# Attention and a max-out feed-forward layer in one kernel: the down product of the last two tiles by Strassen's algorithm, with the output turned

## The chip, the cores and the metric

The kernel runs on one core of one Trainium2 chip. The metric is the device time in microseconds (us) of the whole program, the median of several executions. A profile comes from one execution of its own, with every instruction's engine, start and duration; its span runs from the first to the last instruction.

The engines: TensorE (PE, with its weight loads as PEld) multiplies into PSUM banks; VectorE (DVE), ScalarE (ACT) and GpSimd (POOL) do element-wise work; SyncE (SP) issues the DMA transfers here.

## What is computed

```python
scores = scale * np.matmul(q, k.transpose(0, 1, 3, 2))      # batch 8, heads 8, seq 576, head_dim 64
...
scores = np.where(masks[None, :, :, :], scores, -1000000000.0)   # windows of 32, plain or dilated by 4
...
attn_out = np.matmul(attn, v)                                # softmax in between
x = np.ascontiguousarray(attn_out.transpose(0, 2, 1, 3)).reshape(B * S, H * D)   # 4608 x 512
h = np.maximum(np.maximum(x @ w1, x @ w2), x @ w3)           # 512 -> 768: the up products
return (h @ w_out).astype(np.float32)                        # 768 -> 512: the down product
```

All inputs and the output are float32.

## The kernel before

**Three passes.** A float32 operand is kept as a high part (fp32r, rounded by a cast) and a low part (the operand less its high part). A product takes three passes: high x high, high x low, low x high. So each operand of a product costs a cast (mostly on ScalarE, the helper `copy`, L425) and a subtraction (VectorE or GpSimd, the helper `tt`, L453). Every product below has its factor 3 from this.

**Tiles.** The 4608 tokens go through the feed-forward layer in three tiles of 512 tokens (`plain`) and four of 768 (`fast`), which begin at tokens 1536, 2304, 3072 and 3840. Attention, for 32 units of one batch and a pair of heads, runs ahead of the tiles in between; its output waits in `raw`, a ring of 1152 tokens. It is over before the down product of tile 2304 ends. The scores are the matmuls of L881, the masks L919, the transposes L985, the values matmuls L1041.

**Up product of a fast tile.** Its three weight matrices are multiplied by Strassen's algorithm (Winograd's form), in nine items (feature pair f, matrix g), each of seven products P1 to P7. The halves are: the 512 inputs in two, the tokens in two of 384, the features in pairs of 128. The seven operands on the x side (R11, T1, T2, R21, R22, T3, T4: four quarters and differences) are cast and subtracted once for a tile into `xop`, a part of the tile `wup`. The sums on the weight side were made once, lie in DRAM as `kept_a` and `kept_b`, and are loaded for each item into three buffers `sa` and four buffers `sb` (parts of `wup` and `xs`) that are given out in turn. A product is 6 matmuls (L1415) with a 128x128 block of the weights stationary and 384 tokens moving. The results are combined and taken into the maximum in `hf` (768 features in six blocks of 128 partitions, 768 tokens as columns), by copies on ScalarE and additions and maxima on VectorE.

**Down product of a fast tile.** For six blocks of 128 tokens, `down_part` casts and subtracts 128 columns of all six feature blocks of `hf` into one of two buffers `h` (768 columns wide; the subtraction is mostly on GpSimd). Then 18 matmuls (L1163: six feature blocks, three passes) run with the block of h stationary and the 512 columns of `wdn` (w_out, split when it is loaded) moving, into one bank. ScalarE copies the bank to `o` (L425), and SyncE stores it (L1195). The first block, tokens 384 to 511, is opened ahead of the tile's last up product: four of its feature blocks stand before that product, so that TensorE has work while the last features are finished. The very last bank is copied in two halves, by ScalarE and VectorE.

**What sets the order.** Every step is given to a planner (`Plan`) with a cost for each engine that may do it, its dependences and its buffers. The planner runs through the program with these costs and writes out one order for each engine: feed-forward matmuls follow each other as written, results of the feed-forward layer come first on the other engines (a due time of -1000), and everything else has a due time counted back from the matmul that needs it. Buffers of some kinds are given in turn. The engines then run these orders strictly, each instruction waiting for semaphores.

## Time and profile before

| | |
|---|---|
| median of 3 executions | 657.51 us (656.93 to 657.53) |
| the profiled execution | 657.69 us, of which the span is 655.9 us |
| TensorE busy, share of the span | 644.7 us, 98% |
| VectorE, ScalarE, GpSimd busy | 64%, 46%, 38% |
| DMA | 137.48 MB, 210 GB/s on average |
| mean granted TensorE clock | 0.996 of full speed |

Busy time of TensorE counts a matmul from its first column to its modelled end, so that neighbours overlap; the distance between the starts of matmuls that follow each other tells what one costs. The chain that ended last is followed back from the last instruction: at each step to what released it, or to the instruction before it on its engine. An execution's own time is compared with its own span; the times of two kernels are compared by their medians.

### The profile page before, as it was taken

Reading aid. Unit: us, or ns where it says so; the run is one execution under the profiler, and the core shown is the slowest. Engines: PE = TensorE matmul, PEld = TensorE weight load, DVE = VectorE, ACT = ScalarE, POOL = GpSimd, SP = SyncE. Lnnn points to the kernel's source line nnn. Section 1 sums busy time; section 2 is a strip of 40 time slices with the busy share of each in tenths; the row PEclk is TensorE's granted clock in tenths of the full one; section 3 lists DMA queues with packets and bytes.
Section 4 is the critical chain, followed back from the end, with each engine's and each line's share of the span. In section 5 each row is a group of like instructions: output and inputs, shape, how many; then the busy total and the mean of one; then the engine's idle time right before and its main releaser. Section 6 shows DMA issues by size and latency. Waiting matters only on the chain.

```text
span 655.9 us, 15914 instructions
## 1 busy us (share of the span) xinstructions
PE 644.7 (98%) x6243; PEld 565.8 (86%) x6243; DVE 417.6 (64%) x1224; ACT 300.4 (46%) x909; POOL 248.4 (38%) x284
## 2 busy tenths in 40 slices
PE   8999999999999999999999999999999999999997
PEld 4577778888778878899998899998899998999986
DVE  5688975888969998698877378837033365143320
ACT  4366457545466834535635565235422244322222
POOL 5455585888879943302304222004200014000032
PEclk9899999999999999999999999999999999999999
DMA  9899925546366535987874367674167763377001
GB/s 346 305 363 347 371 80 177 180 146 209 98 217 226 191 129 193 336 304 281 306 243 176 110 225 274 235 253 164 65 226 257 254 229 110 106 279 263 11 33 64
DMA packets 39723, 137.48 MB, mean 210 GB/s; under 512 B 4064, under 2 KB 10720, under 8 KB 35040
## 3 DMA queue, kind: packets, MB, share of 16 engines
q1 hardware_dynamic: 39648, 136.46, 59.1%
q8 instruction: 49, 0.80, 0.5%
q14 instruction: 26, 0.21, 0.1%
HBM read 110.49 MB, written 25.95 MB: 208 GB/s over the span
## 4 chain that ended last, share of the span: by engine, by line
PE 79%; DVE 8%; POOL 5%; DMA 3%; issue 2%; ACT 1%; SPq 0%; POOLq 0%; DVEq 0%; ACTq 0%
PE ffn L1415 40%; PE ffn L1163 20%; PE ffn L1242 10%; PE pair L1041 2%; PE pair L881 2%; POOL s L453 2%; DMA st<-in_w_up_dram 2%; DVE PT L985 2%; DVE W L453 1%; PE pair L627 1%; DMA kept_b<-c 1%; POOL c L453 1%; DVE xs L453 1%; DVE hf L453 1%; DMA fk<-in_qk_p_dram 1%
## 5 line engine op out<-in xcount | busy, mean ns | idle before, releaser
L1415 PE MATMUL ffn<-wup 128*128 128x384 f32 x1026 | 188.1, 335 | 0.0
L1415 PEld LDWEIGHTS ffn<-wup 128*128 128x128 f32 x1026 | 178.5, 188 | 0.8
L453 POOL TENSOR_TENSOR h<-hf,h 128x768 fp32r<-128x768 f32 (+2 forms) x36 | 67.9, 1887 | 267.7 <-ACT h L425 102.5
L1242 PE MATMUL ffn<-xs,wup 128*128 128x512 f32 x648 | 152.1, 393 | 1.4 <-DVE hf L453 1.4
L1163 PE MATMUL ffn<-wdn,h 128*128 128x512 f32 x648 | 152.8, 392 | 0.1
L1242 PEld LDWEIGHTS ffn<-xs,wup 128*128 128x128 f32 x648 | 120.3, 188 | 28.4 <-DVE hf L453 1.8
L1163 PEld LDWEIGHTS ffn<-wdn,h 128*128 128x128 f32 x648 | 120.5, 188 | 25.4 <-DVE h L453 0.6
L985 DVE STREAM_TRANSPOSE PT<-W 32x256 f32<-32x256 f32 (+2 forms) x288 | 109.5, 380 | 16.1 <-PE pair L1041 6.5
L453 DVE TENSOR_TENSOR hf<-ffn,hf 128x384 f32<-128x384 f32 (+1 forms) x108 | 64.8, 600 | 74.1 <-PE ffn L1415 68.4
L1415 PE MATMUL ffn<-wup,xs 128*128 128x384 f32 x486 | 93.8, 335 | 0.0
L931 ACT ACTIVATE W<-W,mx 128x96 f32<-128x96 f32 (+2 forms) x240 | 86.5, 364 | 15.7 <-DVE mx L919 14.3
L1415 PEld LDWEIGHTS ffn<-wup,xs 128*128 128x128 f32 x486 | 85.0, 188 | 0.4
L425 ACT COPY ffn<-ffn 128x384 f32<-128x384 f32 x34 | 15.7, 463 | 90.4 <-PE ffn L1415 90.3
L425 ACT CAST h<-hf 128x768 fp32r<-128x768 f32 (+4 forms) x43 | 30.8, 732 | 54.6 <-PE ffn L1163 34.5
L931 ACT ACTIVATION_READ_ACCUMULATOR W<-W,mx 128x1 f32 (+1 forms) x240 | 45.5, 190 | 0.0
L919 DVE CUSTOM_DVE_ANT_0 W<-pair,steps 128x96 f32<-128x96 f32 (+1 forms) x188 | 36.0, 252 | 13.3 <-PE pair L881 12.0
L453 POOL TENSOR_TENSOR W<-W,sm 128x768 f32<-128x768 f32 (+2 forms) x39 | 37.0, 954 | 19.3 <-DVE sm L960 18.8
L453 DVE TENSOR_TENSOR wup<-raw,wup 128x768 fp32r<-128x768 f32 x28 | 32.8, 1182 | 13.3 <-ACT wup L425 13.2
L955 POOL TENSOR_TENSOR sm<-sm,small_c 128x8 f32<-128x8 f32 (+2 forms) x48 | 12.1, 260 | 65.6 <-ACT W L931 65.0
L453 DVE TENSOR_TENSOR hf<-ffn,u 128x384 f32<-128x384 f32 x12 | 6.7, 558 | 45.9 <-PE ffn L1415 45.8
L425 ACT COPY u<-ffn 128x384 f32<-128x384 f32 x36 | 17.2, 478 | 37.0 <-PE ffn L1415 36.8
L453 POOL TENSOR_TENSOR s<-s,c 128x512 fp32r<-128x512 f32 (+1 forms) x27 | 32.4, 1207 | 3.9 <-ACT c L425 2.7
(113 smaller groups left out, 634.4 us busy)
## 6 DMA issues: line engine op xcount, KB each, us to landing
wup<-kept_a SPq DMA_DIRECT2D x36, 1024.0 KB, 6.0
xs<-kept_b SPq DMA_DIRECT2D x27, 768.0 KB, 4.2
st<-in_w_up_dram SPq DMA_DIRECT2D x18, 512.0 KB, 7.2
out_dram<-o SPq DMA_DIRECT2D x34, 256.0 KB, 2.0
k<-in_qk_d_dram SPq DMA_DIRECT2D x12, 648.0 KB, 4.8
k<-in_qk_p_dram SPq DMA_DIRECT2D x12, 592.0 KB, 5.8
wup<-kept_b SPq DMA_DIRECT2D x9, 768.0 KB, 4.2
kept_a<-wup SPq DMA_DIRECT2D x9, 512.0 KB, 8.3
```

The lines of the kernel that those rows point to most:

```text
L425: nc.scalar.copy(dst, src)
L453: (nc.vector if eng == "dve" else nc.gpsimd).tensor_tensor(dst, a, b, op=op)
L627: nc.tensor.matmul(half(j)[32 * r : 32 * r + nq, 64 * n : 64 * n + 64], qb.t[d, q0 : q0 + nq], kb.t[d, ko + k0 : ko + k0 + 64], start=Fals ...
L881: nc.tensor.matmul(banks[j].t[o : o + nq, 96 * m : 96 * m + nk], kb.t[d, q0 : q0 + nq], kb.t[d, k0 : k0 + nk], start=True, stop=True,)
L919: nc.vector.tensor_tensor_reduce(W.t[rows, a], banks[j].t[rows, 96 * m : 96 * m + nk], mask_of(m)[rows], -0.125, 3e38, ALU.add, ALU.min, m ...
L931: nc.scalar.activation(W.t[rows, a], W.t[rows, a], AF.Exp, bias=mx.t[rows, n : n + 1], scale=-1.0, accum_out=sm.t[rows, n : n + 1],)
L955: nc.gpsimd.tensor_tensor(d, d, eps_c[rows].broadcast_to([d.shape[0], n]), op=ALU.add)
L985: plan.add({"dve": dve(32 * n) + 0.02}, lambda _: nc.vector.transpose(dst(), src()), [*deps, blank], [W, PT])
L1041: nc.tensor.matmul(pv[z].t[64 * j : 64 * j + 64, q : q + c1 - c0], v.t[d, j, y], PT.t[d, 576 * j + 96 * x + c0 : 576 * j + 96 * x + c1], s ...
L1163: nc.tensor.matmul(bank.t, hb.t[:, hz, f], wdn[f].t[:, wz], start=(f == 0 and m == 0), stop=(f == NF - 1 and m == 2), skip_group_check=True,)
L1242: nc.tensor.matmul(bank.t, wup[:, j, wz, 128 * c : 128 * c + 128], xs[:, xz, c, first : first + n], start=(m == 0 and c == EARLY[0]), stop ...
L1415: nc.tensor.matmul(bank.t[:, :n], wb.t[:, w : w + 128], xop[o][:, xz, c], start=start and not m and not c, stop=m == 2 and c == 1, skip_gr ...
```

## The change

For the tiles at 3072 and 3840 (`TURNED`) the down product is done by the same algorithm, with seven products:

- The 768 features are halved by taking the even blocks (0, 2, 4) against the odd ones (1, 3, 5): three pairs q. The 512 outputs are halved in 256 (two blocks e of 128), the tokens in two of 384 (k).
- The weights are stationary and the tokens move: a step is one product for one pair q, 2 blocks e x 3 passes = 6 matmuls of 384 columns. The output has its 512 columns on partitions, so it is turned, goes to an output of its own (`out_t`, 512 x 1536), and is turned back on the host.
- The operands on the h side are cast and subtracted one pair at a time (128 x 384) into `hop`: four buffers, two in each of the two buffers `h`, given in turn. The cast is on ScalarE or GpSimd, the subtraction on VectorE alone. Of the differences, T1 is made in place in `hf`; T2, T3 and T4 are made in buffers that attention no longer needs (`W`, `PT`).
- The sums on the side of the down weights are made once: pairs 0 and 1 after the up products of tile 1536, pair 2 after those of tile 2304 (`down_sums`), stored in DRAM (`kept_d`), and loaded four times for a tile (P5, P6, P3, P7) into the buffers `sb`. P1, P2 and P4 use quarters of `wdn` as they are.
- Two steps of P1 stand before the tile's last up product, as four feature blocks did.
- For tile 3840 the differences of the x side are made apart (`apart`): two of the four go to places of the ring whose tokens are done with, and the first three wait for no operand to be split; its x subtractions may no longer go to GpSimd.
- In the last tile P4 is done for one output block after the other, and the last bank is copied in two halves of 192 columns.

```diff
+TURNED = (3072, 3840)
...
+    KEPT["h"] = [const.tile([128, 2, NF, 128], F32R, name=f"h_{i}") for i in range(2)]
+    KEPT["hop"] = [
+        t.rearrange("p z f n -> p (z f n)")[:, 768 * i : 768 * i + 768].rearrange("p (z n) -> p z n", z=2)
+        for t in KEPT["h"]
+        for i in range(2)
+    ]
...
+    def down_sums(q, after):
...
+        f1, f2 = both(0, c1), both(1, c2)
+        t1 = made(s12, a, c1, z, c2, z, ALU.add, [f1, f2])
+        t3 = made(s34, a, c1, a, c1, z, ALU.subtract, [f1])
+        t2 = made(s12, z, s12, a, c1, a, ALU.subtract, [t1])
+        t4 = made(s34, z, c2, a, s12, z, ALU.subtract, [t2])
...
+        def changed(o, q, x, y, deps):
+            dst = at(0, q, 1) if o == "T1" else SLOTS[3 * q + int(o[1]) - 2]
+            st = plan.add({"dve": dve(n)}, lambda e: tt(e, dst, x, y, ALU.subtract), deps, both=True)
...
+        def split(o, q, src, deps):
+            hop = buf("hop", f"{o}_{t0}_{q}")
+            h = plan.add(
+                {"act": act(n, False), "pool": pool1(n)}, lambda e: copy(e, hop.t[:, 0], src), deps, [hop]
+            )
+            l = plan.add(
+                {"dve": dve(n)},
+                lambda e: tt(e, hop.t[:, 1], src, hop.t[:, 0].bitcast(F32), ALU.subtract),
+                [h],
+                [hop],
+                both=True,
+            )
...
+            def fn(_):
+                for e in es:
+                    for m, (wz, hz) in enumerate(((0, 0), (0, 1), (1, 0))):
+                        nc.tensor.matmul(
+                            bank[e].t[:, :n],
+                            weights(wz, e),
+                            hop.t[:, hz],
...
+            prev = step(prev, "P1", nq - 1, top, True, [])
+            s1 = [copied(f"ds1{t0}_{e}", "o", top[e], prev) for e in E]
...
+            for q in Q:
+                prev = step(prev, "P5", q, mid, True, [])
+            s5 = [copied(f"ds5{t0}_{e}", "tmp", mid[e], prev) for e in E]
+            for q in Q:
+                prev = step(prev, "P6", q, top, False, [x[1] for x in s1])
+            u2 = [copied(f"du2{t0}_{e}", "tmp", top[e], prev) for e in E]
+            for q in Q:
+                prev = step(prev, "P3", q, mid, False, [x[1] for x in s5])
+            for e in E:
+                added(0, 1, e, mid[e], u2[e][0], [prev, u2[e][1]])
+            for q in Q:
+                prev = step(prev, "P7", q, top, False, [x[1] for x in u2])
+            read = [added(1, 1, e, top[e], s5[e][0], [prev, s5[e][1]]) for e in E]
...
+            for q in Q:
+                prev = step(prev, "P2", q, side, True, [])
+            for e in E:
+                added(0, 0, e, side[e], s1[e][0], [prev, s1[e][1]])
...
+            for es in ((0,), (1,)) if last else ((0, 1),):
+                for q in Q:
+                    prev = step(prev, "P4", q, top, False, read, es)
...
             l = plan.add(
-                {"dve": dve(2 * n), "pool": pool(2 * n)},
+                {"dve": dve(2 * n)} if t0 - 2 * n in TURNED else {"dve": dve(2 * n), "pool": pool(2 * n)},
                 lambda e: tt(e, xop[o][:, 1], src, xop[o][:, 0].bitcast(F32), ALU.subtract),
...
+            d1 = sub(block(0, 1), block(0, 1), block(0, 0), [*of(0, 0), *of(0, 1)])
+            d2 = sub(place(0), block(1, 1), block(0, 1), [d1, *of(1, 1), *before])
+            d3 = sub(place(1), place(0), block(0, 0), [d2])
...
+            qs = {2: range(2), 1: range(2, NF // 2)}.get((TURNED[0] - t0) // n, ())
+            plan.kind = "s"
+            kept_down = [*kept_down, *(x for q in qs for x in down_sums(q, ups_end[t0]))]
```

How the order on the engines changes, at three places. Up to the down product of tile 1536 it is the same on all of them. Lines of the helpers move by some numbers (`tt` L453 to L466, the up matmuls L1415 to L1723); the matmuls of `down_part` stay L1163 before and are L1307 after for the turned tiles. `ffn_91` to `ffn_94` before, `ffn_93` to `ffn_96` after, are the same four banks; `h_89` and `h_90` are the two buffers `h`, `W_83` to `W_86` and `PT_87` attention's.

TensorE at the start of the down product of tile 3072, before (x3 is one feature block, x6 one product):

```order
L1415 MATMUL ffn_93<-wup,xs 128x384 x6
L1163 MATMUL ffn_94<-wdn_1227,h_384_6265 128x512 x3
L1163 MATMUL ffn_94<-wdn_1255,h_384_6265 128x512 x3
L1163 MATMUL ffn_94<-wdn_1272,h_384_6265 128x512 x3
L1163 MATMUL ffn_94<-wdn_1296,h_384_6265 128x512 x3
L1415 MATMUL ffn_93<-wup,xs 128x384 x6
L1163 MATMUL ffn_94<-wdn_1304,h_384_6265 128x512 x3
L1163 MATMUL ffn_94<-wdn_1388,h_384_6265 128x512 x3
```

and after, the two opening steps, the last up product, the third step of P1 and the first of P5:

```order
L1723 MATMUL ffn_95<-wup,xs 128x384 x6
L1307 MATMUL ffn_96<-h_89,wdn_1230 128x384 x3
L1307 MATMUL ffn_93<-h_89,wdn_1230 128x384 x3
L1307 MATMUL ffn_96<-h_89,wdn_1274 128x384 x3
L1307 MATMUL ffn_93<-h_89,wdn_1274 128x384 x3
L1723 MATMUL ffn_95<-wup,xs 128x384 x6
L1307 MATMUL ffn_96<-h_90,wdn_1306 128x384 x3
L1307 MATMUL ffn_93<-h_90,wdn_1306 128x384 x3
L1307 MATMUL ffn_94<-h_90,xs 128x384 x3
L1307 MATMUL ffn_95<-h_90,xs 128x384 x3
```

108 matmuls of 512 columns become 126 of 384, in two banks at a time instead of one.

VectorE at the same place, before: the last maxima of the up product, with the x side of tile 3840 (`wup<-raw`: x subtractions, `raw<-raw`: differences):

```order
L453 TENSOR_TENSOR hf<-s_3072_8_6383,hf 128x384
L453 TENSOR_TENSOR wup<-raw,wup 128x768
L453 TENSOR_TENSOR h_384_6265<-hf,h_384_6265 128x256
L453 TENSOR_TENSOR raw<-raw 128x2x384
L453 TENSOR_TENSOR hf<-ffn_93,hf 128x384
L453 TENSOR_TENSOR raw<-raw 128x2x384
L453 TENSOR_TENSOR wup<-raw,wup 128x768
```

and after, from the last up product's maximum on (`hf<-ffn_95,hf`): the four differences of the last pair (T1 in `hf`, T2 and T3 in `W_86`, T4 in `PT_87`), then T1's subtraction, T2's three, and two x subtractions:

```order
L466 TENSOR_TENSOR hf<-ffn_95,hf 128x384
L466 TENSOR_TENSOR hf<-hf 128x384
L466 TENSOR_TENSOR W_86<-hf 128x384
L466 TENSOR_TENSOR W_86<-W_86,hf 128x384
L466 TENSOR_TENSOR PT_87<-hf,W_86 128x384
L466 TENSOR_TENSOR h_89<-hf,h_89 128x384
L466 TENSOR_TENSOR h_90<-W_83,h_90 128x384
L466 TENSOR_TENSOR h_90<-W_84,h_90 128x384
L466 TENSOR_TENSOR h_89<-W_86,h_89 128x384
L466 TENSOR_TENSOR wup<-raw,wup 128x768 x2
```

From here to the end of the down product there stand, in this order: 3 subtractions of R22, an x subtraction, 3 of T3, 2 results, 2 of R21, an x subtraction, 2 results, the third of R21, 3 of T4, 2 results, the x side's last difference and its subtraction. In tile 3840 the queue is the same without the x side, and there T1's subtraction of the last pair stands right behind the last up product's maximum.

VectorE after the down product of tile 1536, after the change: the sums of pair 0, and the first of pair 1 ahead of the first mask instruction of the next attention units (L932). Before, that instruction followed directly on the first row:

```order
L466 TENSOR_TENSOR wup<-raw,wup 128x768
L466 TENSOR_TENSOR dc_0_4817<-wdn_1230 128x512
L466 TENSOR_TENSOR dc_0_4839<-wdn_1258 128x512
L466 TENSOR_TENSOR ds_0_4889<-dc_0_4817,dc_0_4839 128x256
L466 TENSOR_TENSOR ds_0_4889<-ds_0_4889,dc_0_4817 128x256
L466 TENSOR_TENSOR ds_0_4892<-dc_0_4817 128x256
L466 TENSOR_TENSOR ds_0_4892<-dc_0_4839,ds_0_4889 128x256
L466 TENSOR_TENSOR ds_0_4892<-ds_0_4892,dc_0_4839 128x512
L466 TENSOR_TENSOR ds_0_4889<-ds_0_4889,dc_0_4817 128x512
L466 TENSOR_TENSOR dc_1_4961<-wdn_1274 128x512
L932 ISA W_83,mx_4921<-pair_91,steps 128x96
```

The other seven of pair 1 stand among the mask instructions, and TensorE reaches the next scores one up product later and the next values two up products later.

## Rows read from the trace of the kernel before

**Rows 1.** The page's first section: engine, busy us (share), instructions.

```profile
PE 644.7 (98%) x6243; PEld 565.8 (86%) x6243; DVE 417.6 (64%) x1224; ACT 300.4 (46%) x909; POOL 248.4 (38%) x284
```

**Rows 2.** Chain that ended last, in order of time: start us, us, what.

```profile
471.77 64.48 PE ffn L1415 x372
...
540.03 21.77 PE ffn L1163 x96
561.80 64.48 PE ffn L1415 x372
626.28 2.73 PE ffn L1163 x12
629.01 1.04 PE ffn L1415 x6
630.06 21.77 PE ffn L1163 x96
651.90 0.38 ACT o L425
652.30 0.42 DVE o L429
```

**Rows 3.** Busy time in four stretches (columns in the first row).

```profile
core 0: us, PE busy (x) PEld busy (x) DVE busy (x) ACT busy (x) POOL busy (x), PEclk, DMA share, GB/s
376.00:444.00 68.00, 68.00 (x547) 67.22 (x546) 45.28 (x144) 31.68 (x108) 10.39 (x17) 1.00 0.71 245
444.00:472.00 28.00, 28.00 (x215) 23.44 (x214) 13.89 (x15) 12.90 (x25) 10.54 (x5) 1.00 0.31 110
536.09:561.64 25.55, 25.55 (x116) 21.33 (x115) 13.83 (x15) 10.17 (x15) 10.44 (x5) 1.00 0.33 118
626.12:652.00 25.88, 25.70 (x115) 21.14 (x114) 2.40 (x5) 7.12 (x12) 9.26 (x5) 1.00 0.14 52
```

**Rows 4.** VectorE by form, 472 to 652: count, busy us, mean ns, idle before.

```profile
L453 DVE TENSOR_TENSOR hf<-ffn,hf 128x384 f32<-128x384 f32 x36 | 20.1, 558 | 54.7 <-PE ffn L1415 54.2
L453 DVE TENSOR_TENSOR wup<-raw,wup 128x768 fp32r<-128x768 f32 x7 | 8.5, 1227 | 4.2 <-ACT wup L425 4.2
...
L453 DVE TENSOR_TENSOR h<-hf,h 128x256 fp32r<-128x256 f32 x2 | 0.8, 422 | 0.5 <-ACT h L425 0.5
```

**Rows 5.** Timeline, VectorE and GpSimd in the two down products: start us, us, instruction.

```profile
538.86 2.47 POOL L453 TENSOR_TENSOR h<-hf,h 128x768 fp32r<-128x768 f32 x1 [20.95 <-DVE h L453]
...
540.07 0.56 DVE L453 TENSOR_TENSOR hf<-ffn,hf 128x384 f32<-128x384 f32 x1 [0.46 <-PE ffn L1415]
540.54 1.60 DVE L453 TENSOR_TENSOR raw<-raw 128x768 f32<-128x768 f32 x1
...
545.00 0.94 DVE L453 TENSOR_TENSOR raw<-raw 128x768 f32<-128x768 f32 x1
...
625.95 0.56 DVE L453 TENSOR_TENSOR hf<-ffn,hf 128x384 f32<-128x384 f32 x1
626.42 0.55 DVE L453 TENSOR_TENSOR s<-ffn,s 128x384 f32<-128x384 f32 x1
627.01 0.56 DVE L453 TENSOR_TENSOR hf<-s,hf 128x384 f32<-128x384 f32 x1
```

**Rows 6.** ScalarE by form, 626.12 to the end: count, busy us, mean ns, idle.

```profile
L425 ACT CAST h<-hf 128x768 fp32r<-128x768 f32 x5 | 4.2, 835 | 11.0 <-PE ffn L1163 8.3 <-issue 2.8
L425 ACT COPY o<-ffn 128x512 f32<-128x512 f32 x5 | 2.9, 582 | 2.7 <-issue 2.7
...
L425 ACT CAST h<-hf 128x256 fp32r<-128x256 f32 x1 | 0.4, 408 | 3.9 <-DVE hf L453 3.9
L425 ACT COPY o<-ffn 128x256 f32<-128x256 f32 x1 | 0.4, 372 | 3.5 <-PE ffn L1163 3.5
```

**Rows 7.** Timeline of VectorE after the down product of tile 1536.

```profile
362.03 1.62 DVE L453 TENSOR_TENSOR wup<-raw,wup 128x768 fp32r<-128x768 f32 x1 [0.90 <-ACT wup L425]
372.95 0.26 DVE L919 CUSTOM_DVE_ANT_0 W<-pair,steps 128x96 f32<-128x96 f32 x1 [9.30 <-PE pair L881]
```

**Rows 8.** The page's DMA issues: count, KB each, us to landing.

```profile
wup<-kept_a SPq DMA_DIRECT2D x36, 1024.0 KB, 6.0
xs<-kept_b SPq DMA_DIRECT2D x27, 768.0 KB, 4.2
```

More of the change, by code (lines that the diff above doesn't have):

```diff
@@ L111, in __init__ @@
         self.next = []
+        self.later = []
         self.left = 0
@@ L151, in add, with follows @@
         return step
+    def follows(self, step, first):
+        first.later.append(step)
+        step.left += 1
     def deadlines(self):
@@ L319, in order @@
                     slots[b.tag].append((b.end + 0.2, b.slot))
-            for n in st.next:
+            for n in (*st.next, *st.later):
                 n.left -= 1
@@ L1523, in fast @@
             else:
-                if i == len(ITEMS) - 1:
+                if i == len(ITEMS) - 1 and t0 in TURNED:
+                    opening, rest = turned_down(t0, done)
+                    prev = opening(prev)
+                elif i == len(ITEMS) - 1:
                     down, stored = opened()
@@ L1527, in fast @@
                         prev = down(h, prev)
-                st = product(k, i, x["top"], False, [x["read"]])
+                ups_end[t0] = st = product(k, i, x["top"], False, [x["read"]])
                 result(f + 1, g, 0, x["top"], None, [st])
+        if t0 in TURNED:
+            return rest(prev)
         for h in range(4, NF):
@@ L1579, in units @@
         )
+        finished.append(s)
+        for st in lent_to:
+            plan.follows(st, s)
         for x in made:
@@ L1687 @@
         args.append(nc.dram_tensor(f"in_{name}_dram", a.shape, mybir.dt.from_np(a.dtype), kind="ExternalInput").ap())
[L1688 removed]
+    nt = TURNED[0]
+    args.append(nc.dram_tensor("out_0_dram", (nt, DM), F32, kind="ExternalOutput").ap())
+    args.append(nc.dram_tensor("out_1_dram", (DM, NT - nt), F32, kind="ExternalOutput").ap())
     with tile.TileContext(nc) as tc:
         tile_dilated_window_attention__then__maxout_ffn(tc, *args)
[L1691 to L1692 removed]
+    r = _run(nc, [arrays], core_ids=[0]).results[0]
+    return np.concatenate([r["out_0_dram"], r["out_1_dram"].T])
```

253 lines of the change are left out of this document (230 added, 23 removed).

## The prediction

> **What bounds the kernel now.** I read the page's first section, then the chain that ended last in order of time, then the windows of the last five stages, then single instructions. TensorE is busy for 98% of the span [rows 1]. The chain, from 471.77 us on, is nothing but matmuls: the 372 up matmuls of one tile, the down product, the next tile's 372, the last down product, and then two copies [rows 2]. In the windows TensorE is busy for the whole length of each stage up to the last, the granted clock is 1.00, and VectorE, ScalarE and GpSimd have room: in the down product of tile 3072 VectorE works 13.83 of 25.55 us [rows 3]. So the end is set by how many matmuls there are and how far apart they start, as long as no other engine is late. Two rates come out of the chain. Down: 96 matmuls of 512 columns in 21.77 us, 226.8 ns each. Up: 372 matmuls of 384 columns in 64.48 us, 173.3 ns each. Each is about 13 ns above its columns at the 2.4 GHz level.
>
> **What the change takes from TensorE.** The down product of a 768-token tile was 6 blocks of 128 tokens x 6 feature blocks x 3 passes = 108 matmuls of 512 columns: 108 x 226.8 = 24.50 us. It becomes 7 products x 3 feature pairs x 2 output blocks x 3 passes = 126 matmuls of 384 columns. These have the form of the up matmuls (128x128 weights stationary, 384 tokens moving), so I give them that row's rate: 126 x 173.3 = 21.84 us. The gain is 2.66 us for a tile and **5.32 us** for the two [rows 2]. The Trainium skill, page "TensorE: Matmul & The Clock Gate", section "Back-to-back issue gap", gives N/2.4 + 2.5 ns for an isolated matmul at full clock. By it the two sums would be 108 x 215.8 and 126 x 162.5 ns and the gain 5.66 us. The rows here show 11 ns more per matmul at both widths, and the new form has more matmuls, so I keep the rows.
>
> **The last copy and store.** Before, the last bank is copied in two halves of 256 columns, 372 ns on ScalarE and then VectorE, and stored. Now the halves have 192 columns. 512 columns take 582 ns and 256 take 372 [rows 6], 0.82 ns a column, so 64 columns less save about 0.05 us on each engine; one starts when the other ends [rows 2]. Gain **0.1 us**; the stores behind it stay as they were.
>
> **What it adds beside TensorE, in the down product of tile 3072.** Per tile 21 operands (7 products x 3 pairs) are each cast on ScalarE and subtracted on VectorE, 12 differences are made on VectorE, and 6 results are added there. GpSimd's five or six wide subtractions go; at the same time the x operands of tile 3840 are prepared, and now all their subtractions stand on VectorE, in its queue between the new ones. I count that queue by what stands in it. A 384-column subtraction lasts 0.56 us [rows 4]; one that needs nothing of its predecessor starts 0.47 us after it, one that does 0.59 us after it [rows 5]. A 768-column one is 0.94 us alone and 1.60 beside GpSimd [rows 5]; GpSimd is nearly empty now, so I take 0.94. Let t = 0 be the first down matmul.
> First place: the operand T1 of the last pair. The 18 matmuls of t = 0 to 3.12 end the last up product; VectorE reads it 0.04 to 0.2 us later [rows 2, 5]. Then stand its maximum, four differences (T1 to T4), and only then T1's subtraction: five starts of 0.47 to 0.59 and 0.56 for the last, so it is ready at 6.1 to 6.8. TensorE, 36 matmuls on, wants it at 6.24. Stall 0 to 0.6.
> Second place: R21 of the last pair. Until it stand 16 more short instructions (7.5 to 9.4 us) and 4 x subtractions (3.8 us): ready between 17.4 and 20.0. TensorE wants it after 108 matmuls, at 18.72 plus the first stall. Together **0 to 1.3 us; I take 0.5**, nearer the low end since most of the sixteen don't need their predecessor.
> ScalarE has some 20 casts and 8 copies there. A cast of 256 columns takes 408 ns and one of 768 takes 835 [rows 6], so 384 about 0.52 us; with copies of the same order that is 15 of 23 us. One buffer's way round (TensorE lets go, cast 0.52, subtraction 0.56, handoffs some 0.5) is 1.6 us, and with four buffers three others cover 3 x 1.04 us.
>
> **The last tile.** The same, without x operands, and T1's subtraction stands right behind the maximum: 3.2 + 0.47 + 0.56 = 4.2, wanted at 6.24. Up to R21's last there are 17 short instructions, 8 to 10 us, and 18.72 us for them. VectorE waits for TensorE here, not the other way round. I put **0.1** (0 to 0.3) for handoffs.
>
> **The sums of the down weights.** Three times VectorE makes two sums and two low parts of 512 columns and four differences of 256. From the 256-, 384- and 768-column rows [rows 4, 5] that is 4 x 0.69 + 4 x 0.42 = 4.4 us, two of them during and after the down product of tile 1536, one in that of tile 2304. The cover: VectorE stood idle for 9.30 us before 372.95 us [rows 7], which takes the first; the third has the 14 us that VectorE leaves of the window 444 to 472 [rows 3]. The second stands among the mask instructions of attention, and the values matmuls that follow now stand two up products later on TensorE. If that shift is enough it costs nothing; without it, up to the 4.4 us less the 2.1 us of the two products. I take **0.1** (0 to 1).
> **Transfers.** 12 stores of 256 KB, and per tile four loads of 768 KB in the buffers of kept_b, which land in about 4.2 us [rows 8]. The last of the four can start at 3.1 and is wanted at 13.5; the next tile's first kept_b load waits for a buffer until 7.3 or so and is wanted after 23. On SyncE's queue they stand among the next tile's kept_a loads, which are not wanted before that tile starts. Nothing of this is on the path.
>
> **The sum.** -5.32 - 0.1 + 0.5 + 0.1 + 0.1 = -4.7 us. The profiled execution took 657.69 us, 0.18 above the median of 657.51; from the median I forecast **652.8**.
>
> **The rivals.**
> No stall at all, 5.32 + 0.1 = 5.4 less: **652.1**. For it: every short VectorE instruction at 0.47, and no TensorE wait in any of the windows up to 626 now [rows 3]. Against: the order puts four differences ahead of the subtraction that TensorE wants first. 20%.
> The forecast, 652.4 to 653.6: 53%.
> VectorE is held up by GpSimd. A subtraction of two SBUF inputs took 1.60 us instead of 0.94 while GpSimd ran, and GpSimd's own took 2.47 [rows 5]; the x subtractions' mean of this stretch is 1.23 [rows 4]. If that stays, the four before the second place cost 0.66 us more each, 2.6 in all, on top of 0.5: **655.4**. The Trainium skill, page "SBUF — State Buffer", section "SBUF: two separate sides", says that the two engines share a port pair and that whoever starts first keeps it for a whole instruction while the other blocks. By that rule the x casts still on GpSimd would do this; the trace agrees so far that both stretch. Against the rival: GpSimd keeps only four such casts, at the very start of the stretch. 13%.
> The sums push attention: the values matmuls are reached before their operands, 1 to 2 us: **654.3**. 10%.
> Slower than before: four operand buffers are too few. If VectorE's queue once falls more than three steps (3.1 us) behind, every step pays the buffer's way round of 1.6 instead of 1.04 us. The gain is gone after 5.4 / 0.56 = 10 of the 42 steps; over one whole tile's 21 steps it is 11.8 us more: **663.9**. For it: the x subtractions come in groups of two. Against: a group is 1.9 us, less than three steps. 4%.
>
> **Range and chances.** 651.9 to 655.4 leaves out the slower rival, the upper ends of the two before it, and a little below. A difference under 0.2% (1.3 us) can't be told from none. Faster by more means under 656.2: 0.91. Within it: 0.05. Slower: 0.04.
>
> **What the profile would show.** Down matmuls: 252 of 384 columns, 173 ns apart. From the first of them to the next tile's first up matmul 22.9 us plus stalls instead of 25.54 (chain); in the last tile 22.9 with none. TensorE's waits: entries on VectorE's h subtractions in tile 3072 at T1 and R21. VectorE there nearly full, GpSimd nearly empty, x subtractions at 0.94 us. Wrong would be: a spacing over 190 ns in the new matmuls, waits of several us in the last tile, or new waits of TensorE between 346 and 536 us.

## The result and the profile after

The changed kernel took 651.43 us (median of six runs, 650.44 to 652.53) against 658.16 us of the kernel before in the same comparison. The ratio is 0.9899, with a 95% interval of 0.9882 to 0.9915: 6.7 us less, 5.6 to 7.8. The forecast was 652.8, and its range began at 651.9, so the direction was right and the first comparison fell half a microsecond below the range. Three more comparisons, told below, gave ratios of 0.9919, 0.9928 and 0.9928. The medians over all runs of these comparisons, and of the one more in which only the kernel before ran beside other versions, are 652.10 us for the changed kernel (23 runs) and 657.39 for the kernel before (102 runs): 5.3 us less.

The profiled execution took 651.02 us, its span 649.2. The first section of its page (engine, busy us, share, instructions) answers [rows 1]:

```profile
PE 637.4 (98%) x6279; PEld 568.5 (88%) x6279; DVE 465.8 (72%) x1324; ACT 310.8 (48%) x941; POOL 231.0 (36%) x278
```

TensorE has 36 matmuls more and is busy 7.3 us less; VectorE took over work and is busy 48 us longer. The end of the chain (start us, us, what) answers [rows 2]:

```profile
470.09 64.48 PE ffn L1723 x372
534.57 2.11 PE ffn L1307 x12
536.68 1.06 PE ffn L1723 x6
537.74 19.98 PE ffn L1307 x114
557.72 64.51 PE ffn L1723 x372
622.22 2.11 PE ffn L1307 x12
624.33 1.06 PE ffn L1723 x6
625.39 20.04 PE ffn L1307 x114
...
645.45 0.33 ACT dc L438
...
645.80 0.36 DVE dc L442
```

It is still nothing but matmuls. The up products of a tile are unchanged (64.48 us). The down product of tile 3072, from its first matmul to the next tile's up products, takes 557.72 - 534.57 = 23.15 us. Before, it began here:

```profile
536.26 2.73 PE ffn L1163 x12
```

and took 561.80 - 536.26 = 25.54 us. The down product of the last tile takes 23.21 instead of 25.55 up to its last matmul. Behind that stand 3.8 us to the end of the span, where 4.1 stood before. Together these places give 5.0 us.

The windows of the two down products (columns as in [rows 3]) show what took over:

```profile
core 0: us, PE busy (x) PEld busy (x) DVE busy (x) ACT busy (x) POOL busy (x), PEclk, DMA share, GB/s
...
534.57:557.72 23.15, 23.15 (x134) 22.95 (x133) 20.63 (x39) 12.31 (x25) 0.83 (x1) 1.00 0.77 257
622.22:645.45 23.23, 23.20 (x133) 22.88 (x131) 15.98 (x32) 11.77 (x24) 0.00 (x0) 1.00 0.26 89
```

In tile 3072 VectorE went from 13.83 to 20.63 us, nearly the whole stretch, and GpSimd from 10.44 to 0.83. TensorE still has no gap to speak of.

The two spans differ by 655.9 - 649.2 = 6.7 us. Where is the rest? A mark helps: the start of the 108 up matmuls of tile 1536 in the chain. Up to it every engine runs the same rows in the same order in both kernels. The mark in the profile before and in the one after:

```profile
280.88 18.92 PE ffn L1415 x108
278.96 18.92 PE ffn L1723 x108
```

So 1.92 us of the difference between these two profiles lie in a part of the program that the change does not touch. (The stretch between the mark and tile 3072 takes 0.24 us back: -1.92 - 5.03 + 0.24 = -6.71.) The first question for the experiments was whether the change does something in that early part. Some expectations name other places of it: the first up matmul of tile 1536 lies 8.9 us ahead of the mark, the piece of 24 up matmuls 6.06 us.

### The profile page after: what moved, and what is told of

Its sections match the earlier page's. It is cut to its first block, busy times and chain, and to the rows that moved or that the text cites. A ratio compares the mean times of both kernels' runs of the same rounds, so it can differ in the third digit from the quotient of the medians.

```text
span 649.2 us, 16232 instructions
## 1 busy us (share of the span) xinstructions
PE 637.4 (98%) x6279; PEld 568.5 (88%) x6279; DVE 465.8 (72%) x1324; ACT 310.8 (48%) x941; POOL 231.0 (36%) x278
## 4 chain that ended last, share of the span: by engine, by line
PE 88%; DVE 6%; POOL 2%; issue 2%; DMA 1%; ACT 1%; SPq 0%; POOLq 0%; DVEq 0%
PE ffn L1723 41%; PE ffn L1521 15%; PE ffn L1442 15%; PE ffn L1307 7%; PE pair L894 3%; PE pair L1054 2%; PE ffn L1943 2%; DVE PT L998 2%; DVE W L466 1%; PE pair L640 1%; DMA kept_b<-c 1%; POOL s L466 1%; PE pair L761 1%; DVE W L932 1%; DVE hf L466 1%
## 5 line engine op out<-in xcount | busy, mean ns | idle before, releaser
L1723 PE MATMUL ffn<-wup 128*128 128x384 f32 x1026 | 188.2, 335 | 0.0
L1723 PEld LDWEIGHTS ffn<-wup 128*128 128x128 f32 x1026 | 178.4, 188 | 0.8
L466 DVE TENSOR_TENSOR hf<-ffn,hf 128x384 f32<-128x384 f32 (+1 forms) x108 | 64.8, 600 | 67.4 <-PE ffn L1723 60.7
L1442 PE MATMUL ffn<-wdn,h 128*128 128x512 f32 x432 | 103.2, 394 | 0.3 <-DVE h L466 0.3
L1442 PEld LDWEIGHTS ffn<-wdn,h 128*128 128x128 f32 x432 | 79.9, 188 | 17.5 <-DVE h L466 0.8
L1723 PE MATMUL ffn<-wup,xs 128*128 128x384 f32 x486 | 93.7, 334 | 0.0
L1723 PEld LDWEIGHTS ffn<-wup,xs 128*128 128x128 f32 x486 | 85.0, 188 | 0.2
L466 POOL TENSOR_TENSOR h<-hf,h 128x768 fp32r<-128x768 f32 (+2 forms) x24 | 45.0, 1874 | 103.7 <-ACT h L438 60.1
L438 ACT CAST h<-hf 128x384 fp32r<-128x384 f32 (+5 forms) x52 | 32.3, 632 | 44.4 <-DVE hf L466 18.9
L466 POOL TENSOR_TENSOR W<-W,sm 128x768 f32<-128x768 f32 (+2 forms) x39 | 37.0, 955 | 16.7 <-DVE sm L973 16.2
L932 DVE CUSTOM_DVE_ANT_0 W<-pair,steps 128x96 f32<-128x96 f32 (+1 forms) x188 | 36.1, 253 | 4.3 <-PE pair L894 2.7
L466 DVE TENSOR_TENSOR wup<-raw,wup 128x768 fp32r<-128x768 f32 x28 | 30.4, 1098 | 9.2 <-ACT wup L438 9.2
L466 POOL TENSOR_TENSOR s<-s,c 128x512 fp32r<-128x512 f32 (+1 forms) x27 | 33.1, 1233 | 3.9 <-ACT c L438 2.7
L438 ACT COPY hf<-ffn 128x384 f32<-128x384 f32 (+1 forms) x41 | 21.6, 527 | 24.6 <-PE ffn L1521 13.8
```

The source lines that it names most:

```text
L438: nc.scalar.copy(dst, src)
L466: (nc.vector if eng == "dve" else nc.gpsimd).tensor_tensor(dst, a, b, op=op)
L932: nc.vector.tensor_tensor_reduce(W.t[rows, a], banks[j].t[rows, 96 * m : 96 * m + nk], mask_of(m)[rows], -0.125, 3e38, ALU.add, ALU.min, m ...
L1442: nc.tensor.matmul(bank.t, hb.t[:, hz, f], wdn[f].t[:, wz], start=(f == 0 and m == 0), stop=(f == NF - 1 and m == 2), skip_group_check=True,)
L1723: nc.tensor.matmul(bank.t[:, :n], wb.t[:, w : w + 128], xop[o][:, xz, c], start=start and not m and not c, stop=m == 2 and c == 1, skip_gr ...
```

## The experiments

**Is the early gain the change's?** The kernel before, unchanged:

> The kernel before, unchanged, against itself. The two traces agree with the forecast from 346 us on: each turned tile is 2.4 us shorter, the end 0.25, the middle 0.2 longer, which makes about -4.85. But 1.7 to 1.9 us of the measured -6.65 lie in the first 270 us, where every engine runs the same rows in the same order. Theory chance: the start waits for loads, and these differ between executions; then this kernel against itself may stray by 0.2 to 0.3% either way, and the first up matmul of tile 1536 (271.94 us before, 270.03 after) moves by a us or two from one profile to the next. Theory layout: the start is faster because h stands in other memory or the program has more buffers in DRAM; then this kernel gives a ratio within 0.1% of 1 and its first up matmul of tile 1536 stands near 271.9 again.

It measured 657.06 us, ratio 0.9995 (0.9979 to 1.0011). In its profile the mark stood at 279.39 us, 1.5 us earlier than in the first profile of the same program. So the start of this program can differ by that much without any change to it.

The memory of the change alone:

```
-        "h": (2, [128, 2, NF, 128], F32R),
...
+    KEPT["h"] = [const.tile([128, 2, NF, 128], F32R, name=f"h_{i}") for i in range(2)]
...
+    kept_d = spill.tile([128, 4, NF // 2, 2, 256], F32, name="kept_d")
```

> The kernel before with the change's memory alone: h as two fixed buffers instead of a pool's, and the DRAM buffer of the down-weight sums reserved and unused. No instruction is added or moved. Theory layout: 1.7 us faster than before, ratio 0.9974, first up matmul of tile 1536 near 270.0. Theory chance: the same time as before, within 0.15%, and the start of its profile anywhere between 270 and 272.

656.46 us, ratio 0.9989 (0.9972 to 1.0007), mark at 280.87: by itself this decides nothing, since the time leaves room for a gain of up to 1.8 us. The changed kernel again:

> The changed kernel, unchanged. Theory layout: -6.6 us again (ratio 0.9899), with the first up matmul of tile 1536 near 270.0 again. Theory chance: between -4.6 and -5.6 us (ratio 0.9915 to 0.993), the -1.7 of the first comparison having been luck.

652.45 us, ratio 0.9919 (0.9898 to 0.9940), 5.1 us below the median beside it; mark at 279.38. The ratio is where theory chance put it.

**One tile alone.** Tile 3072's down product is left as before, and the x subtractions beside it may go to GpSimd again; the sums stay as changed (the second line of the edit, not shown):

```
-TURNED = (3072, 3840)
+TURNED = (3840,)
...
```

> The changed kernel with tile 3072's down product as before; only the last tile is turned. The down-weight sums, the memory and the x differences of the last tile stay as changed. By the steps of the forecast: 2.4 us for the down product, 0.25 for the end, less 0.2 for the sums: -2.45 against before if the start has no systematic gain (ratio 0.9963), -4.2 if it has (ratio 0.9936). Against the changed kernel of this call it is 2.4 us slower by both. The down stretch of tile 3072 takes 25.5 us again.

654.96 us, ratio 0.9966 (0.9951 to 0.9981): 2.2 us less than before (1.2 to 3.2), forecast 2.45. The chain shows 25.54 us again for the down product of 3072 and 23.21 for the last. So each tile's down product is shorter only where it is turned, and the two gains add up.

**The sums of the down weights.** The repeat of the changed kernel had a wait that its first profile lacked. Its chain around 376 us (start us, us, what):

```profile
375.75 0.63 ACT dc L438
...
376.40 0.37 SPq L1196
...
376.81 0.02 SPq L872
...
376.86 6.17 DMA k<-in_qk_d_dram
...
383.17 1.27 PE pair L894 x64
```

Read it from below. The scores matmuls (L894) start late, by 0.8 us in the waits, because their load of k takes 6.17 us to land. That load (L872) stands on SyncE's queue behind a store of the sums (L1196), which waited for ScalarE's cast of the sums (dc). The prediction had put transfers at nothing, and had called a new wait of TensorE between 346 and 536 us a sign of being wrong. To see what the sums cost, they were made and stored without anything that uses them, with h in fixed buffers, and both down products as before:

> The kernel before with the change's additions ahead of the turned tiles alone: h in fixed buffers and the sums of the down weights, made and stored and never read; both down products as before. Forecast: 0.1 us (0 to 1) slower than before. Theory traffic: the stretch from the first up matmuls of tile 1536 to the long piece of 372 of tile 3072 is 197.1 to 198.5 us instead of 196.95, with TensorE waits on a k load or on a copy that waits for a tmp buffer still being stored; so 0.2 to 1.5 us slower than before, ratio 1.0003 to 1.0023. Theory layout: the start is faster by 1.7 us and the kernel 0.5 to 1.5 us faster than before.

658.53 us, ratio 1.0021 (1.0008 to 1.0034): 1.4 us slower than before (0.5 to 2.2). The chain says where:

```profile
377.37 0.67 POOL dc L440
...
378.06 6.11 DMA kept_d<-dc
...
384.25 0.49 ACT u L438
```

Here it is not k. ScalarE's copy u of an up product's bank needs one of the five tmp buffers, and the sums keep theirs until the store has landed, 6.11 us after its issue. TensorE waits 0.9 us for u, and the stretch from the mark to tile 3072 is 1.2 us longer than before (472.73 - 280.62 = 192.11 against 190.89).

Then the sums were moved behind the up matmuls of tile 2304, where no k is loaded:

```
-            qs = {2: range(2), 1: range(2, NF // 2)}.get((TURNED[0] - t0) // n, ())
+            qs = {1: range(NF // 2)}.get((TURNED[0] - t0) // n, ())
```

> All three pairs of down-weight sums are made after the up matmuls of tile 2304 instead of two of them after those of tile 1536; nothing else is changed. In the repeat of the changed kernel the scores at 383 us waited 0.8 us for a load of k: its issue stands on SyncE behind a store of sums that waits for ScalarE, and took 6.2 us to land beside the eight stores of 256 KB. Theory traffic: without them there, the time from the first up matmuls of tile 1536 (the chain's piece of 24) to the long piece of 372 of tile 3840's predecessor is as in the kernel before, 196.95 us, instead of 197.2 to 198.0, and no TensorE wait on a k load stands in that stretch: 0.2 to 1.0 us faster than the changed kernel, 651.0 to 652.2 if that takes 652.2. Rival: the loss in the middle is not the sums but the other order of values matmuls and up products, or chance; then the stretch stays at 197.2 or more. A second rival: VectorE is now too full between 444 and 480 us and TensorE waits there for the h maxima of tile 3072: the stretch becomes longer by 1 us or more.

659.45 us, ratio 1.0028 (1.0012 to 1.0043). This failed, and the whole gain was gone. The half that was forecast came true: from the mark to the up products of tile 3072 it is 190.89 us, as in the kernel before (190.89). But none of the rivals that I wrote down is what followed. The chain from there:

```profile
470.69 5.22 PE ffn L1723 x30
...
477.31 6.86 DMA kept_d<-ds
484.32 0.49 ACT u L438
...
484.86 3.42 PE ffn L1723 x18
...
488.67 1.07 ACT dc L438 x2
489.74 5.88 DMA kept_d<-dc
495.72 0.49 ACT u L438
...
496.25 46.59 PE ffn L1723 x258
```

It is the tmp buffers again. Twelve of them are wanted for the sums, and each is held until its store has landed, 6.86 and 5.88 us after issue for the two in the chain, while every group of seven up products wants two or three. ScalarE's copy u waits, TensorE's bank is not let go, and the 372 up matmuls take 542.84 - 470.69 = 72.15 us instead of 64.48. VectorE, which I suspected, does not stand in the chain. Not all of the 7.7 us are waits: TensorE stood idle for u for 1.01 and 3.83 us, and behind the longer idle its granted clock was lower for a while, 0.63 on the mean of 3.75 us (columns as in the windows above):

```profile
496.25:500.00 3.75, 3.75 (x14) 3.75 (x15) 3.58 (x7) 0.31 (x1) 0.00 (x0) 0.63 0.75 288
```

The last 258 up matmuls take 46.59 us where 258 x 173.3 ns would be 44.71: 1.9 us of the loss. With two of the pairs there instead of three, and the order of VectorE's differences from the next experiment:

```
...
+            qs = {2: range(1), 1: range(1, NF // 2)}.get((TURNED[0] - t0) // n, ())
```

> As the T1 kernel, and one of the two pairs of sums of tile 1536's stage is made in that of tile 2304, so that one stands in the first and two in the second. With all three in the second TensorE lost 8 us in tile 3072's first up products: ScalarE's copies of these waited for tmp buffers until the stores of the sums had landed, 6 to 7 us each. Theory buffers: two pairs need eight of the five tmp buffers; the second pair's stores are issued at about 470 us and land near 476 to 480, and the copies wait again, 1 to 5 us in all, so that it is slower than the changed kernel although the stretch before 443 us is as short as in the kernel before. Rival: the third pair alone was too many; then there is no wait and the kernel is 0.2 to 1 us faster than the changed one.

652.59 us, ratio 0.9936 (0.9917 to 0.9955); the changed kernel beside it had 0.9928 (0.9909 to 0.9947), so the two can't be told apart. The mechanism of theory buffers holds, at the low end of its size; that the kernel is slower than the changed one is not shown. The stretch up to 470 us is 190.98 us long, the up products of 3072 take 65.49 us, 1.0 more than undisturbed, and a store of the sums stands in the chain ahead of u once. What the early stretch gave, the late one took.

**T1 in the down product of tile 3072.** The forecast had put a wait at the operand T1. TensorE's timeline of the changed kernel there (start us, us, instruction):

```profile
537.58 1.22 PE L1307 MATMUL ffn<-h,wdn 128*128 128x384 f32 x6
538.64 3.47 PE L1307 MATMUL ffn<-h,xs 128*128 128x384 f32 x18
541.95 3.28 PE L1307 MATMUL ffn<-h,wup 128*128 128x384 f32 x18
545.07 6.41 PE L1307 MATMUL ffn<-h,xs 128*128 128x384 f32 x36
551.31 6.41 PE L1307 MATMUL ffn<-h,wdn 128*128 128x384 f32 x36
```

The starts count: T1's 18 matmuls (538.64) last 3.31 us until the next start, the groups behind them 3.12 or 6.24, which is 173.3 ns each. (A matmul's start in a timeline lies 0.16 us ahead of its place in the chain, which counts from the modelled end of the matmul before; the first down matmul is at 534.41 here and at 534.57 there.) VectorE's timeline beside it:

```profile
537.78 0.56 DVE L466 TENSOR_TENSOR hf<-ffn,hf 128x384 f32<-128x384 f32 x1 [0.47 <-PE ffn L1723]
...
540.37 0.55 DVE L466 TENSOR_TENSOR h<-hf,h 128x384 fp32r<-128x384 f32 x1
```

These are the last up product's maximum and, behind the four differences, T1's subtraction (h<-hf,h). It ends at 540.92, and the waits list this for the weight load:

```profile
PEld ffn L1307 <- DVE h L466: 0.2, 1, 0.2
```

Two experiments put T3 and T4 behind that subtraction, the first with the later sums, the second with the sums in place:

```
-        t3 = [changed("T3", q, t2[q][0], at(0, q, 0), [t2[q][1]]) for q in Q]
+        t3 = [changed("T3", q, t2[q][0], at(0, q, 0), [t2[q][1], made["T1", q][1]]) for q in Q]
...
```

> As the kernel with the later sums, and besides the differences T3 and T4 wait for T1's subtraction of their pair, so that on VectorE the subtraction of T1 of the last pair comes ahead of them. In the changed kernel that subtraction ended 6.5 us after the first down matmul of tile 3072 and TensorE's weight load waited 0.20 us for it, the only recorded wait of the two down products. Theory order: the wait is gone and the stretch from the first down matmul of tile 3072 to the next tile's first up matmuls is 22.95 instead of 23.15 us. Rival: what is late next (T2's subtractions, now with fewer differences made ahead, or T3's) takes its place and the stretch stays at 23.1 or more.

> The changed kernel, its sums where they were, with T3 and T4 of a pair made after T1's subtraction of that pair. With the later sums this took the down stretch of tile 3072 from 23.33 to 23.01 us. Theory order: 23.15 becomes 22.9 to 23.0 here too, no weight load of the two down products waits, the last tile is unchanged at 23.2; 0.2 us on the whole, which the times alone can't show. Rival: another operand takes the place of T1 and the stretch stays at 23.1 or more.

The first measured 660.49 us, ratio 1.0044 (1.0027 to 1.0061), and loses its gain to the sums as the one without it; its stretch is 23.01 us against 23.33. The second measured 652.72 us, ratio 0.9935 (0.9915 to 0.9956), and its stretch is 23.23 us, above the 23.0 of theory order. The groups show where the time is:

```profile
539.81 3.36 PE L1307 MATMUL ffn<-h,xs 128*128 128x384 f32 x18
543.01 3.34 PE L1307 MATMUL ffn<-h,wup 128*128 128x384 f32 x18
```

T1's group lasts 3.20 us, as it does in the two kernels with this order that made sums late (3.18 and 3.19), against 3.31 or 3.32 in the changed kernel's profiles and the one with sums late alone. But the next group takes 3.18 here, and the one after that 6.36 instead of 6.24. Of the four profiles of the changed kernel the third has the same 3.18 and 6.36, and the others have not. So the order saves 0.12 us, and another 0.18 come and go between profiles with no wait on record; what they are stays open.

**Four operand buffers or three.** The prediction's rival by which the change would have made the kernel slower said that four buffers are too few. With three:

```
-    ]
+    ][:3]
```

> The changed kernel with three operand buffers instead of four. The slower rival said that with too few buffers each step of 6 matmuls costs the way round of 1.6 instead of 1.04 us: up to 11.8 us a tile. The forecast's arithmetic gives two other buffers that cover 2 x 1.04 = 2.08 us against 1.6, so nothing in the last tile (23.2 us again) and in tile 3072 at most 1 us at each place where VectorE has two wide x subtractions (1.9 us) in a row, of which there are one to three: 23.2 to 26 us there. If the whole way round is longer than 2.08 us, both tiles are longer by the difference for every step, 21 times.

654.94 us, ratio 0.9953 (0.9935 to 0.9972), 2.8 us above the median of the changed kernel in its own four comparisons. The down product of 3072 takes 24.45 us (536.13 to 560.58) and the last 23.85, together 1.9 us more than in the changed kernel. TensorE's timeline in 3072:

```profile
546.21 1.14 PE L1307 MATMUL ffn<-h,wup 128*128 128x384 f32 x5 [0.38 <-DVE h L466]
...
553.20 1.14 PE L1307 MATMUL ffn<-h,xs 128*128 128x384 f32 x5 [0.40 <-DVE h L466]
```

Two stops, each behind a row of other work on VectorE (two wide x subtractions, then one and two additions), and one more in the last tile; between them the pace is the usual one. Here a shortage of buffers costs at the place where VectorE is held up, not at every step after it, so the rival's 11.8 us for a tile was the wrong price even where its mechanism occurs.

**GpSimd and VectorE.** The x subtractions of tile 3840 go to GpSimd, where some of them stood before:

```
-                {"dve": dve(2 * n)} if t0 - 2 * n in TURNED else {"dve": dve(2 * n), "pool": pool(2 * n)},
+                {"pool": pool(2 * n)} if t0 - 2 * n in TURNED else {"dve": dve(2 * n), "pool": pool(2 * n)},
```

> The changed kernel with the x subtractions of tile 3840 on GpSimd, as many of them stood there before, instead of on VectorE. Rival contention (in the prediction 655.4): the two engines hold each other up on wide operands; then the operand subtractions on VectorE beside GpSimd take 0.8 to 1.5 us instead of 0.56, R21's of the last pair misses its time (it was ready 18.4 us after the first down matmul and wanted at 19.0), and the stretch is longer by 0.5 to 2.6 us. Other theory: VectorE is freed of 7 times 0.95 us and that outweighs it; then the stretch is 22.9 to 23.15 us as in the changed kernel, and VectorE's busy time in it falls from 20.6 us to some 14.

655.27 us, ratio 0.9962 (0.9947 to 0.9977), 3.2 us above the changed kernel's median of the other comparisons. The down product of 3072 takes 561.97 - 535.20 = 26.77 us, 3.6 more. Both engines' timelines there:

```profile
534.27 0.57 DVE L466 TENSOR_TENSOR ffn<-ffn,u 128x384 f32<-128x384 f32 x1 [0.55 <-PE ffn L1723]
...
535.92 1.80 DVE L466 TENSOR_TENSOR hf<-s,hf 128x384 f32<-128x384 f32 x1
537.26 2.14 POOL L466 TENSOR_TENSOR wup<-raw,wup 128x768 fp32r<-128x768 f32 x1
537.65 2.18 DVE L466 TENSOR_TENSOR h<-hf,h 128x384 fp32r<-128x384 f32 x1
539.37 2.15 POOL L466 TENSOR_TENSOR wup<-raw,wup 128x768 fp32r<-128x768 f32 x1
```

While GpSimd works off its row of subtractions, a VectorE subtraction of two SBUF inputs that takes 0.56 us alone takes 1.80 to 2.18, about as long as one of GpSimd's (2.14). One that reads a TensorE bank (ffn) still takes 0.57. The Trainium skill, page "SBUF — State Buffer", section "SBUF: two separate sides", says that a VectorE operation with two SBUF inputs and a GpSimd operation that reads SBUF take the same port pair in turn, each for its whole instruction; these rows agree with it. So putting these subtractions on VectorE is part of what the change gains: VectorE nearly full is better here than two engines in each other's way.

**The start once more.** By then the marks stood 0.8 us earlier on the mean in the ten profiles of kernels whose output lies in two DRAM tensors, as the change needs it, than in the four others. So the kernel before got that memory too, first the split output alone, then all of the change's memory, beside the kernel before and the changed kernel:

```
...
-    args.append(nc.dram_tensor("out_0_dram", (NT, DM), F32, kind="ExternalOutput").ap())
+    args.append(nc.dram_tensor("out_0_dram", (3072, DM), F32, kind="ExternalOutput").ap())
+    args.append(nc.dram_tensor("out_1_dram", (NT - 3072, DM), F32, kind="ExternalOutput").ap())
...
```

> The kernel before with its output in two DRAM tensors, split at token 3072, as the changed kernel has it; no instruction is added or moved. In the profiles so far the 108 up matmuls of tile 1536 begin at 278.9 to 280.6 us (mean 279.6) in ten kernels with the split output and at 279.4 to 280.9 (mean 280.4) in four without it, though all run the same rows up to there. Theory output: where the buffers of the output lie changes the start's loads; this kernel is then 0.5 to 1 us faster than before (ratio 0.9985 to 0.9992) and the mark stands near 279.6. Theory chance: ratio 0.9995 to 1.0005 and the mark anywhere from 279 to 281.

> The kernel before with all of the change's memory: the output in two tensors, h in fixed buffers, the DRAM buffer of the sums reserved and unused. No instruction is added or moved. Theory output or memory: 0.5 to 1 us faster than before, the mark near 279.6. Theory chance: as before within 0.4 us, the mark anywhere from 279 to 281.

> The kernel before once more, unchanged, to pool its times with those of before for a narrower comparison with the two others of this call. By both theories a ratio within 0.1% of 1.

> The changed kernel, a fourth time. Behind the mark its three profiles took 370.2 to 371.1 us against 375.0 for the kernel before, a gain of 3.9 to 4.8. Theory chance: 4.0 to 5.3 us faster than before. Theory output or memory: 4.9 to 5.8 us, and the two memory kernels of this call account for the 0.5 to 1 us on top.

The two memory kernels took 657.89 and 657.30 us, ratios 1.0011 (0.9997 to 1.0025) and 0.9999 (0.9984 to 1.0013), the unchanged one 657.10, ratio 1.0007 (0.9993 to 1.0022). Memory gives nothing that 24 runs show. The changed kernel took 652.15 us, ratio 0.9928 (0.9913 to 0.9943). The other repeat of the changed kernel, which ran beside the T1 and sums kernels, agrees:

> The changed kernel a third time, beside the kernel before. If the start of the program is chance, its gain lies between 4.0 and 5.7 us as in the last comparison (5.1 of medians) and not at 6.7. If something in the start is truly faster, it is 6 us or more. The k load at 383 us may wait or not (0 to 0.8 us).

652.06 us, ratio 0.9928 (0.9909 to 0.9947). The marks of all profiles of these programs, what follows them to the end of the span, in us, and TensorE's mean granted clock from 16 to 24 us:

| kernel | mark | mark to end | clock, 16 to 24 us |
|---|---|---|---|
| before | 280.88 | 375.0 | 0.79 |
| before again, twice | 279.39, 280.92 | 375.0, 375.1 | 1.00, 0.79 |
| before with h and sums memory | 280.87 | 375.2 | 0.79 |
| before with split output | 280.29 | 375.3 | 0.79 |
| before with all of the memory | 278.86 | 375.0 | 1.00 |
| changed, first | 278.96 | 370.2 | 1.00 |
| changed, three repeats | 279.38, 279.63, 280.91 | 371.1, 370.6, 370.3 | 1.00, 1.00, 0.79 |

The first column strays over 2 us, whatever the kernel. The second is steady and tells the change's worth: 3.9 to 5.1 us, 4.6 in the mean.

The last column goes with the first: all five marks from 280.29 up stand with the lower clock, all five up to 279.63 with the full one. In the two profiles of the unchanged kernel with the marks 280.88 and 279.39, one row of TensorE's timeline from that stretch is

```profile
18.20 2.87 PE L1623 MATMUL ffn<-blank_b 128*128 128x512 bf16 x9
18.29 2.12 PE L1623 MATMUL ffn<-blank_b 128*128 128x512 bf16 x9
```

The same nine matmuls take 2.87 us where the granted clock falls to 0.50 of full speed (1.2 GHz) from 20 to 22 us, and 2.12 where it stays at 1.00 (2.4 GHz). In both TensorE had stood idle for 1.9 us shortly before. The eight other profiles of the experiments fit less neatly: with the lower clock their marks lie from 279.77 to 280.62, with the full one from 278.94 to 280.57. Over all 18 the difference of the means is 1.0 us. That the clock moves the mark was not tested, and why it falls in some executions is open. It goes far to explain the 0.8 us from which these last experiments started: three of the four profiles without the split output had the lower clock there, and two of the ten with it.

## Why the prediction was right and where it failed

**The step that failed.** The mechanism and the path are as forecast, but the sum has terms only for the turned tiles, the end and the sums of the down weights, so all that runs before the mark entered it as nothing. In the first two profiles that part differed by -1.92 us with the same instructions in the same order, and the lower granted clock (0.79 against 1.00 from 16 to 24 us) was on the side of the kernel before. The terms of the forecast make -5.03 + 0.24 = -4.79 us in the same two profiles, against -4.7. So the first comparison left the range through the start of the program. As far as the repeats and the memory kernels show, that is luck of the execution and not a gain of the change; the range had no room for it.

**What bounds the kernel: right.** TensorE's matmuls, their number and their spacing. All of the gain behind the mark stands where the chain was forecast to shrink.

**The 5.32 us of the matmuls: right.** 126 + 6 matmuls at 173.3 ns are 22.88 us; the stretch of 3072 took 23.15 in three of four profiles and 23.36 in one, and the waits and small delays in it are the next points. The new matmuls kept the spacing of the up matmuls, 173.3 ns, as forecast. The formula that the prediction quoted from the Trainium skill (page "TensorE: Matmul & The Clock Gate", section "Back-to-back issue gap") gives an estimate of 162.5 ns at this width; the trace does not agree with it, and the measurement decides.

**The last copy, 0.1: too small by 0.2.** Behind the last matmul 4.07 us became 3.77. The two copies went from 0.80 to 0.69 us as forecast. The rest of it, from the last copy's end to the span's end, went from 3.18 to 3.04.

**VectorE in tile 3072, +0.5: right place, lower end.** T1's last subtraction was forecast for 6.1 to 6.8 us after the first down matmul and ended at 540.92 - 534.41 = 6.51; the wait was 0.20. R21's was forecast for 17.4 to 20.0 and ended at 18.4, wanted at 19.0: no wait. The x subtractions took the 0.95 us of an undisturbed VectorE. The loss was 0.27.

**The last tile, +0.1: measured 0.33** (23.21 against 22.88), with no wait on record. T1's product group and the three behind it run at 176.7 ns instead of 173.3 (12.72 us for 72 matmuls). Why stays open.

**The sums, +0.1 (0 to 1): mis-sized.** From the mark to tile 3072 the kernel before needs 190.9 us, the changed one 191.13, 191.93, 191.25 and 191.16, so 0.2 to 1.0. Alone they cost 1.4 us of time (0.5 to 2.2). The wrong step here is "Nothing of this is on the path", said of the transfers: I looked at who wants the loads of the sums, but not at the k load that is queued behind their stores, nor at the tmp buffers that the stores hold.

**The rivals.** Contention with GpSimd did not occur: a single GpSimd instruction of 0.83 us stands in the stretch, and the x subtractions took 0.95 us. But it is real: the experiment that put it back cost 3.6 us in the stretch, where the prediction had 2.6 for it, and it worked on the short subtractions too, not on the wide ones alone. Too few buffers did not occur with four.

**The range: its low end was too near.** The terms sum to -4.7; behind the mark the profiles show -3.9 to -5.1. The time also holds a start that strays by 2 us between executions, and my low end lay 0.9 us below the forecast. I had used the spread of three runs before (0.6 us), and 102 runs spread over 655.23 to 660.74. The median of 23 runs, 652.10, lies in the range, the first six runs' does not.

The pooled times give 5.3 us and the profiles behind the mark 4.6. A part of the 0.7 between them is the clock. Every run of the changed kernel and 96 runs of the kernel before have their mean granted clock on record. With 0.999 or 1.0 the medians are 652.03 (16 runs) and 656.74 (45 runs), 4.7 us apart, which is what the profiles say; with 0.998 or less they are 652.65 (7 runs) and 658.09 (51 runs), 5.4 apart. The changed kernel had the higher clock in 16 of 23 runs and in all of the first six, the kernel before in 45 of 96. Whether that mix is chance, the runs do not settle.

No version tried here is shown to be faster than the changed kernel.

## What to carry to other kernels

Where TensorE is busy throughout, a change of its work is worth the number of matmuls times the spacing in the chain, and the rest of the work is to find the one or two operands that come late. Of added transfers, ask what is queued behind each store and which buffers it holds until it lands, not only who wants its data. And before a microsecond of an unexpected difference is explained, run the kernel against itself, compare the stretches that the change cannot touch, and compare runs of the same granted clock.

## What was not expected of the hardware

VectorE and GpSimd held each other up instruction by instruction: a subtraction of two SBUF inputs that takes 0.56 us alone lasted 2.18 us beside a GpSimd one of 2.14. The stores of the sums, 256 KB each, landed 2.4 and 2.6 us (medians) after their issue from 465.7 to 470 us of the kernel with all sums late, and 5.9 and 6.9 us at 490 and 477 us, beside the loads of weights. Behind an idle of 3.83 us in the same kernel the granted clock was 0.63 on the mean of the next 3.75 us. And the start of one unchanged program differed by 1.5 us between profiles (marks 279.39 and 280.88), with a mean granted clock of 1.00 and 0.79 from 16 to 24 us.
